# Three Strassen pairs instead of two in the third layer of a fused attention and two-layer network kernel, with two reorderings around them

## Chip, cores, metric

The kernel runs on one core of a Trainium2 chip. The metric is the device time of one execution in microseconds (us); the time before is the median of three runs.

## What is computed

Causal attention over 2 batches, 12 heads, 448 positions and head size 64, followed by two feed-forward networks with 768 inputs and 2048 hidden units on the 896 tokens, all to float32 accuracy:

```python
x = attention(q, k, v)                       # (896, 768)
h = x @ moe_w_in;  g = max(h, 0) + alpha * min(h, 0);  x = g @ moe_w_out
h = x @ moe2_w_in
g = where(h >= 1, h, where(h <= -1, 0, (h + 1) ** 2 / 4))
out = g @ moe2_w_out
```

## The kernel before

The program calls the four matrix products layers one to four: layer one is `moe_w_in`, layer two `moe_w_out`, layer three `moe2_w_in`, layer four `moe2_w_out`. Attention comes first and fills about the first 78 us; then the layers follow one another. The order of every instruction on every engine is written out by hand (`tc.manual_schedule()`), and each engine works off its own list in that order.

**Split operands.** TensorE gets every float32 operand as two parts, a rounded high part and the low part that is left, and does three products for one (high by high, high by low, low by high). A weight tile arrives as raw 8-byte values. GpSimd casts their upper bits to `top` (L209), VectorE joins them with the rest into a float32 tile (`join`, L218), ScalarE copies the high part (`high`, L253), and VectorE subtracts it for the low part (`low`, L257). The split weight goes into one of three `w_split` buffers.

**Layer three.** The 2048 hidden units are 16 f tiles of 128, the 768 inputs are 6 k tiles, and the tokens are two halves b of 448. A plain f tile is 6 x 2 x 3 = 36 matmuls of 448 columns into a pair of PSUM banks (`pair()`, of which there are two in rotation). `ORDER` visits the f tiles as 0, 8, 1, 9, ..., 7, 15; I number the positions of this order 0 to 15, so that positions 2k and 2k + 1 are pair k. During position i the vector engines do three things in the order of the list `ops` in `run_layer`: the activations of position i - 1 (`late[:2]`, the two squares on ScalarE, L339 and L340; `late[2:4]`, the two totals on VectorE, L345, each followed by the split of its result, L324 and L327, or by a store), the weights of position i + 2 (`a`: join, high, load, low), and what stands further back in `late`, the sums over a finished pair.

**Sums of a pair.** Layer four is itself done by Strassen's scheme. `sum_ops` gives for each pair `first` (L383, the matrix S1), `third` (L397) and `second` (L392), which are sums of activations with stores to memory, and a later accumulating DMA for S4. The activations live in six `act` buffers.

**A Strassen pair (`Fold`).** For the pairs in `FOLD[3]`, the two f tiles of a pair are computed by seven products P1 to P7 of 9 matmuls each. P1 runs inside the position before, after its fourth k tile; then P6, P5, P2, P7 and P3 run in one block; P4 runs in the middle of the position after. Bank B holds P1, then P1 + P6, and so on. What a partial sum is still needed for is copied out by ScalarE first: `keep("u1")` after P1, `keep("u2")` after P6, `keep("u5")` from bank D after P5 (all L590). P6 therefore can't begin before u1 is copied, P7 not before u2, P3 not before u5. The sums of weights that these products need are made by `sums12` (L218 join, L546, L547, L550 high, L553 low) and `sums34` (L561, L562, L564, L576), both in the position before. The first Strassen pair also makes the three right-hand sums T4 (L477, L479, L480). The right-hand sums T1 to T4 keep twelve of the 44 on-chip `places` until the last Strassen pair has read them. Where the position before a Strassen pair is the second tile of another pair, `late[4:]` with the deferred sums runs at the very end of its list.

Of the kernel before, what the change touches and what calls it, by code (L numbers as in the profile page):

```python
# [22 lines left out]
def attention_moe_moe_kernel(ctx: ExitStack, tc: tile.TileContext, qk, v, w1, w2, w3, w4, alpha, out):  # L23
# [35 lines left out]
    NPAIR = NF // 2  # L59
    WHOLE = 6  # L60
    ORDER = [f for k in range(NPAIR) for f in (k, NPAIR + k)]
# [3 lines left out]
    NU = len(STEPS) * len(PARTS)  # L65
    QUARTERS = "B11", "B21", "B12", "B22"
    LATE = {1: 0, 2: 0, 3: 0}
    FOLD = {1: (), 3: (2, 5)}
    HALF = KD // 2 * 128
    SIDES = {  # L70
# [259 lines left out]
    def activate(layer, ps, f, b):  # L330
# [11 lines left out]
        def total():  # L342
# [5 lines left out]
            if negate and layer == 3:  # L348
                nc.scalar.mul(g, g, -1.0)
            if f >= NPAIR and b and FOLD[layer]:  # L350
                keep("A22", f - NPAIR, g)
# [13 lines left out]
    def keep(n, k, t):  # L365
        d = sums[n, k] = spill.tile([128, S], F32, tag=f"{n}_{k}", name=f"d{n}_{k}")
        nc.sync.dma_start(out=d, in_=t)
# [6 lines left out]
    def sum_ops(layer, k):  # L374

        tiles = []
        late = layer == 1 and FOLD[1] or layer == 3 and k or k >= NPAIR - 2

        def first():
            g11, g12, g21, g22 = (parts.pop((b, f)) for b in range(NB) for f in (k, NPAIR + k))  # L380
            s1 = act_tile("s1")
            tiles.extend((g11, g21, s1))
            nc.vector.tensor_sub(s1, g21, g22)  # L383
            keep("S4", k, g12)
            lows.extend(split_g(left_tile("S1", k), s1, k + 1 == NPAIR))
            if not late:
                keep("S3", k, g21)
                keep("S2", k, s1)

        def second():  # L390
            g11, _, s1 = tiles
            nc.vector.tensor_add(g11, s1, g11)  # L392
            keep("S2", k, g11)

        def third():
            g11, g21, _ = tiles
            nc.vector.tensor_add(g21, g21, g11)  # L397
            keep("S3", k, g21)

        last = [lambda: add("S4", k, sums["S2", k])] * (k < NPAIR - 2)  # L400
        if late:
            return [first, third, second], [], last
        return [first], [lambda n=n: add(n, k, tiles[0]) for n in ("S2", "S3")], last
# [20 lines left out]
    def pair(pool=None):  # L424
        return (pool or ps_s).tile([128, 2, 512], F32, tag="s", name="ps")
# [4 lines left out]
    def products(ps, ws, src, k, kk, first, last):  # L430

        for part in range(2):
            for b in ps:
                for xp in range(2 - part):
                    nc.tensor.matmul(  # L435
                        ps[b][:, :S],
                        lhsT=ws[:, part, k * 128:(k + 1) * 128],
                        rhs=src[b, kk][:, xp],
                        start=first and part == 0 and xp == 0,
                        stop=last and part == 1,  # L440
                    )
# [184 lines left out]
    def run_layer(layer, late):  # L626

        deferred, last = [], []
        folds = {k: Fold(layer, k, k == max(FOLD[layer])) for k in FOLD[layer]}
        fold, skip = None, 0  # L630
        for i, f in enumerate(ORDER):
            if skip:
                skip = 0
                continue
            if f in folds:
                fold, skip = folds[f], 1
                wts.next()
                for name in ("P6", "P5", "P2"):
                    fold.step(name)
                wts.fill()  # L640
                a, w, w4 = later.ahead(i), fold.second(), fold.split4()
                fourth = [lambda k=k: rights.total("T4", k, nc.gpsimd) for k in range(MH) if f == min(FOLD[layer])]
                c22, c12, c21, c11 = (fold.output(n) for n in ("C22", "C12", "C21", "C11"))
                for ops in ([w4[0], *late[:2], a[0], w4[1], *late[2:4], lambda: fold.keep("u2", "B"), lambda: fold.step("P7")],
                            [a[1], *a[2:], lambda: fold.keep("u5", "D"), lambda: fold.step("P3")],
                            [w[0], c11[0], w[1], *fourth, c22[0], c11[1], *late[4:5], c11[2]]):
                    for op in ops:
                        op()
                late, pending = [*c12, *late[5:], *c22[1:], *deferred], last
                deferred, last = [], []  # L650
                continue
            if layer == 1 and f in early:
                ws, ps = early.pop(f)
                products(ps, ws, x_t, KD - 1, KD - 1, False, True)
                wts.run(wts.load())
            else:
                ws, t = wts.next(), pair()
                ps = {b: t[:, b] for b in range(NB)}
                if layer == 3 and i == 0:
                    for b in range(NB):  # L660
                        ks = [(k + MH * b) % KD for k in range(KD)]
                        for k in ks:
                            products({b: t[:, b]}, ws, x_t, k, k, k == ks[0], k == ks[-1])
                else:
                    for k in range(KD):
                        if k == MH and fold:
                            fold.step("P4")
                        if k == MH + 1:
                            if i + 1 < NF and ORDER[i + 1] in folds:
                                folds[ORDER[i + 1]].start()  # L670
                                folds[ORDER[i + 1]].step("P1")
                        products(ps, ws, x_t, k, k, k == 0, k == KD - 1)
            if wts.n_used > 1:
                wts.fill()
                if i + 1 < NF and ORDER[i + 1] in folds:
                    new = folds[ORDER[i + 1]]
                    a, b = new.sums12(), new.sums34()
                    ops = [*late[:2], a[0], *late[2:4], a[1], lambda: new.keep("u1", "B"), *a[2:], *b, *late[4:]]
                else:
                    a = later.ahead(i - bool(fold))  # L680
                    if fold:
                        ops = [late[0], a[0], late[1], a[1], late[2], *a[2:], *late[3:]]
                    else:
                        ops = [*late[:2], a[0], *late[2:4], a[1], *late[4:5], *a[2:], *late[5:]]
                for op in ops:
                    op()
                if fold:
                    wts.fill()
                    a = later.ahead(i)
                    now, deferred, last = sum_ops(layer, fold.k)  # L690
                    for op in [a[0], c21[0], a[1], c21[1], *a[2:], now[0]]:
                        op()
                    deferred = [*now[1:], *pending, *deferred]
                    fold = None
            for kind, name in SIDES[layer].get(i, ()) if FOLD[layer] else ():
                for k in range(MH):
                    getattr(rights, kind)(name, k)
            late = [op for two in zip(*(activate(layer, ps[b], f, b) for b in range(NB))) for op in two]
            now, before, deferred, last = [], deferred, last, []
            if f >= NPAIR:  # L700
                now, deferred, last = sum_ops(layer, f - NPAIR)
            late += now + before
        for b in range(NB):
            for m in range(KD):
                places.put(f"x{b}", m)
        return late + deferred + last

    class Strassen:
# [9 lines left out]
        def __init__(self, layer):  # L718
            self.layer = layer
            self.f, self.ws, self.bank, self.u = {}, {}, {}, {}  # L720
            self.names = ("S2", "S4", "S3") + ("A22",) * bool(FOLD[layer - 1])

# [362 lines left out]
    with tc.manual_schedule():  # L1085
# [132 lines left out]
        late = []  # L1218
        for layer in (1, 3):
            later = Strassen(layer + 1)  # L1220
            later.run(run_layer(layer, late))
            late = []
# [44 lines left out]
```

## Time and profile before

| | |
|---|---|
| median of three runs | 516.12 us (513.93 to 519.12) |
| profiled execution, its time | 515.88 us |
| profiled execution, its span | 514.1 us |
| TensorE busy | 507.3 us, 99% of the span |
| VectorE busy | 391.0 us, 76% |
| ScalarE busy | 315.4 us, 61% |
| GpSimd busy | 281.6 us, 55% |
| mean granted TensorE clock | 0.997 |

The time of an execution is its span and 1.8 us around it. The span is from the first to the last instruction that the profiler recorded. Matmuls are pipelined: one takes 365 ns from start to end, but the next starts after about 203 ns, so the time of a block is read from the starts of the blocks.

### The profile page before, as it was taken

Reading aid. Unit: us, or ns where it says so; the run is one execution under the profiler, and the core shown is the slowest. Engines: PE = TensorE matmul, PEld = TensorE weight load, DVE = VectorE, ACT = ScalarE, POOL = GpSimd, SP = SyncE. Lnnn points to the kernel's source line nnn. Section 1 sums busy time; section 2 is a strip of 40 time slices with the busy share of each in tenths; the row PEclk is TensorE's granted clock in tenths of the full one; section 3 lists DMA queues with packets and bytes.
Section 4 is the critical chain, followed back from the end, with each engine's and each line's share of the span. In section 5 each row is a group of like instructions: output and inputs, shape, how many; then the busy total and the mean of one; then the engine's idle time right before and its main releaser. Section 6 shows DMA issues by size and latency. Waiting matters only on the chain.

```text
span 514.1 us, 8592 instructions
## 1 busy us (share of the span) xinstructions
PE 507.3 (99%) x2893; PEld 445.8 (87%) x2893; DVE 391.0 (76%) x639; ACT 315.4 (61%) x641; POOL 281.6 (55%) x361
## 2 busy tenths in 40 slices
PE   8999999999999999999999999999999999999997
PEld 4656668999999999999999999898999999999996
DVE  5799876655565599896788689788888898967881
ACT  6899974665556558556643366676677675555531
POOL 7667745667766693325212398586355823480450
PEclk9899999999999999999999999999999999999999
DMA  6646505577778979899344745948568997892211
GB/s 194 191 136 212 158 9 185 178 215 192 164 212 209 225 212 338 279 264 345 122 108 113 211 144 167 222 137 248 177 187 252 290 364 281 244 320 92 73 55 54
DMA packets 46396, 99.97 MB, mean 194 GB/s; under 512 B 6400, under 2 KB 34688, under 8 KB 46352
## 3 DMA queue, kind: packets, MB, share of 16 engines
q1 hardware_dynamic: 35808, 75.69, 43.8%
q0 software_dynamic: 9824, 23.17, 20.4%
q10 hardware_dynamic: 720, 0.56, 0.3%
q8 instruction: 23, 0.38, 0.3%
q14 instruction: 21, 0.17, 0.1%
HBM read 75.09 MB, written 22.48 MB: 190 GB/s over the span
## 4 chain that ended last, share of the span: by engine, by line
PE 87%; DVE 4%; POOL 4%; ACT 3%; issue 2%; DVEq 0%; ACTq 0%; POOLq 0%
PE ps L788 40%; PE ps L435 31%; PE ps L1076 4%; PE ps L997 4%; PE ps L1059 3%; PE ps L522 2%; POOL T L480 2%; PE ps L990 2%; POOL top L209 1%; PE ps L109 1%; DVE g L345 1%; DVE w_split L257 1%; POOL pexp L1034 1%; DVE ps L218 0%; ACT g L339 0%
## 5 line engine op out<-in xcount | busy, mean ns | idle before, releaser
L435 PE MATMUL ps<-x,w_split 128*128 128x448 f32 x1008 | 206.3, 366 | 0.5 <-DVE g L345 0.5
L435 PEld LDWEIGHTS ps<-x,w_split 128*128 128x128 f32 x1008 | 189.1, 188 | 15.9 <-DVE g L345 0.8
L788 PE MATMUL ps<-S,w_split 128*128 128x448 f32 x576 | 117.1, 365 | 0.0
L788 PEld LDWEIGHTS ps<-S,w_split 128*128 128x128 f32 x576 | 108.2, 188 | 8.6
L788 PE MATMUL ps<-A,w_split 128*128 128x448 f32 x432 | 88.2, 365 | 0.0
L788 PEld LDWEIGHTS ps<-A,w_split 128*128 128x128 f32 x432 | 81.1, 188 | 6.4
L327 POOL TENSOR_TENSOR A<-g,A 128x448 fp32r<-128x448 f32 x37 | 49.1, 1334 | 55.6 <-ACT A L324 52.0
L754 ACT CAST w_split<-B 128x768 fp32r<-128x768 f32 x42 | 35.1, 836 | 59.8 <-PE ps L788 25.7
L345 DVE SCALAR_TENSOR_TENSOR g<-ps,g 128x448 f32<-128x448 f32 x62 | 37.9, 622 | 44.2 <-ACT g L335 35.3
L758 DVE TENSOR_TENSOR w_split<-B,w_split 128x768 fp32r<-128x768 f32 x42 | 42.2, 1004 | 19.1 <-ACT w_split L754 18.8
L209 POOL CAST top<-w_raw 128x768 f16<-128x768 bf16 x34 | 48.5, 1428 | 7.3 <-DVE ps L218 6.5
L1034 POOL TENSOR_SCALAR pexp<-pexp,stat 128x384 f32<-128x384 f32 (+3 forms) x79 | 38.9, 513 | 16.5 <-DVE stat L1026 8.3
L1017 ACT ACTIVATE pexp<-pexp,stat 128x128 f32<-128x128 f32 (+3 forms) x84 | 43.7, 524 | 5.6 <-DVE stat L1008 5.2
L195 POOL CAST top<-w_raw 128x256 f16<-128x256 bf16 (+1 forms) x27 | 22.7, 840 | 42.7 <-DMA w_raw<-w 34.8
L335 ACT ACTIVATE g<-ps 128x448 f32<-128x448 f32 x32 | 17.1, 536 | 38.3 <-PE ps L435 38.3
L1008 DVE CUSTOM_DVE_ANT_0 pexp<-ps,mask 128x128 f32<-128x128 f32 (+3 forms) x84 | 33.0, 448 | 6.0 <-POOL ident masks.py:199 3.5
L257 DVE TENSOR_TENSOR w_split<-ps,w_split 128x768 fp32r<-128x768 f32 x27 | 25.8, 955 | 13.7 <-ACT w_split L253 13.4
L218 DVE SCALAR_TENSOR_TENSOR ps<-w_raw,top 128x768 uint32<-128x768 uint32 x27 | 32.4, 1199 | 1.2
L826 POOL DMA_DIRECT2D S<-dS x48 | 26.4, 556 | 9.5 <-PE ps L788 7.4
L842 DVE TENSOR_TENSOR S<-S 128x448 fp32r<-128x448 f32 x48 | 30.3, 656 | 0.0
L324 ACT CAST A<-g 128x448 fp32r<-128x448 f32 x40 | 22.6, 567 | 10.0 <-DVE g L345 8.5
L327 POOL TENSOR_TENSOR S<-s,S 128x448 fp32r<-128x448 f32 x14 | 23.7, 1693 | 7.6 <-ACT S L324 7.6
(127 smaller groups left out, 711.3 us busy)
## 6 DMA issues: line engine op xcount, KB each, us to landing
w_raw<-w SPq DMA_DIRECT2D x29, 767.8 KB, 5.6
w_raw<-w SPq DMA_DIRECT2D x51, 255.8 KB, 5.3
w_raw<-w SPq DMA_DIRECT2D x24, 511.8 KB, 5.2
S<-dS POOLq DMA_DIRECT2D x48, 224.0 KB, 5.4
dS<-g SPq DMA_DIRECT2D x41, 224.0 KB, 4.4
qk<-qk SPq DMA_DIRECT2D x10, 448.0 KB, 3.6
dS<-dS POOLq DMA_DIRECT2D x16, 224.0 KB, 6.1
dS<-g POOLq DMA_DIRECT2D x14, 224.0 KB, 4.9
```

Of the source, the lines that this page charges most:

```text
L209: (side.copy if side is nc.scalar else side.tensor_copy)(d[:, c], src[:, c])
L218: nc.vector.scalar_tensor_tensor(out=w[:, a:b], in0=t.rearrange("p (n two) -> p n two", two=2)[:, c, 0], scalar=13, in1=top[:, c], op0=ALU ...
L257: (side or nc.vector).tensor_sub(s[:, 1, c], w()[:, c], f32(s[:, 0, c]))
L327: nc.gpsimd.tensor_sub(t[:, 1, :], g, f32(t[:, 0, :]))
L345: nc.vector.scalar_tensor_tensor(out=g, in0=ps[:, :S], scalar=floor, in1=g, op0=ALU.max, op1=last, reverse1=negate and layer == 1)
L435: nc.tensor.matmul(ps[b][:, :S], lhsT=ws[:, part, k * 128:(k + 1) * 128], rhs=src[b, kk][:, xp], start=first and part == 0 and xp == 0, st ...
L754: nc.scalar.copy(s[:, 0], w)
L758: nc.vector.tensor_sub(s[:, 1], w, f32(s[:, 0]))
L788: nc.tensor.matmul(ps[:, :S], lhsT=ws[:, part, (at + k - ks[0]) * 128:(at + k - ks[0] + 1) * 128], rhs=left[name, k][:, xp], start=first a ...
L1008: nc.vector.tensor_tensor_reduce(out=self.pexp[p][:, o:o + w], in0=b[:, :w], in1=mask3 if i == 3 else mask[:, 384 - w:], scale=-SCALE, sca ...
L1017: nc.scalar.activation(out=e, in_=e, func=AF.Exp, bias=self.st[p][:, 0, n:n + 1], scale=-1.0, accum_out=self.st[p][:, 1, n:n + 1],)
L1034: nc.gpsimd.tensor_scalar(out=e, in0=e, scalar1=self.st[p][:, 2, n:n + 1], scalar2=1.0, op0=ALU.mult, op1=ALU.mult)
```

## The change

Three edits. The Strassen pairs of layer three become pairs 2, 4 and 6 instead of 2 and 5. In the list of a Strassen pair, the copy of bank B to u2 moves ahead of the low part of S4 and of the two totals of the position before. In the list of a plain position that neither follows nor precedes a Strassen pair, the fifth entry of `late` stays ahead of the load and the low part of the weights only where the position before is a pair's second tile; elsewhere it now comes behind them.

```diff
-    FOLD = {1: (), 3: (2, 5)}
+    FOLD = {1: (), 3: (2,4,6)}
...
-                for ops in ([w4[0], *late[:2], a[0], w4[1], *late[2:4], lambda: fold.keep("u2", "B"), lambda: fold.step("P7")],
+                for ops in ([w4[0], *late[:2], a[0], lambda: fold.keep("u2", "B"), w4[1], *late[2:4], lambda: fold.step("P7")],
                             [a[1], *a[2:], lambda: fold.keep("u5", "D"), lambda: fold.step("P3")],
                             [w[0], c11[0], w[1], *fourth, c22[0], c11[1], *late[4:5], c11[2]]):
...
-                        ops = [*late[:2], a[0], *late[2:4], a[1], *late[4:5], *a[2:], *late[5:]]
+                        n = 5 if i and ORDER[i - 1] >= NPAIR else 4
+                        ops = [*late[:2], a[0], *late[2:4], a[1], *late[4:n], *a[2:], *late[n:]]
```

## Rows read from the trace of the kernel before

**Rows 1.** The page, busy time of each engine.

```profile
PE 507.3 (99%) x2893; PEld 445.8 (87%) x2893; DVE 391.0 (76%) x639; ACT 315.4 (61%) x641; POOL 281.6 (55%) x361
```

**Rows 2.** Chain that ended last, layers three and four: start us, us, what.

```profile
368.08 9.12 PE ps L522 x45
...
408.21 102.16 PE ps L788 x504
```

**Rows 3.** Waits of the weight loads, 293.8 to 410: us in total, times, longest.

```profile
PEld ps L435 <- DVE g L345: 0.8, 1, 0.8
PEld ps L522 <- DVE w_split L553: 0.5, 1, 0.5
PEld ps L522 <- ACT u L590: 0.3, 1, 0.3
```

**Rows 4.** Timeline of PE, 310 to 360: start, us, instructions, count, [idle before].

```profile
324.64 4.20 PE L522 MATMUL ps<-T,w_split 128*128 128x448 f32 x18
328.67 1.99 PE L522 MATMUL ps<-x,w_split 128*128 128x448 f32 x9
330.60 2.09 PE L522 MATMUL ps<-T,S 128*128 128x448 f32 x9
...
339.82 11.11 PE L435 MATMUL ps<-x,w_split 128*128 128x448 f32 x54
351.40 8.78 PE L435 MATMUL ps<-x,w_split 128*128 128x448 f32 x42 [0.47 <-DVE g L345]
```

**Rows 5.** Timeline of ScalarE, first Strassen pair and positions 7 and 8.

```profile
329.55 0.57 ACT L324 CAST A<-g 128x448 fp32r<-128x448 f32 x1 [0.39 <-DVE g L345]
...
348.32 0.63 ACT L339 ACTIVATE g<-ps,half 128x448 f32<-128x448 f32 x1
...
350.11 0.58 ACT L340 ACTIVATE g<-g 128x448 f32<-128x448 f32 x1
...
355.24 0.64 ACT L339 ACTIVATE g<-ps,half 128x448 f32<-128x448 f32 x1 [0.30 <-DVE g L392]
```

**Rows 6.** Timeline of VectorE, position 7, then the second Strassen pair.

```profile
347.73 0.96 DVE L218 SCALAR_TENSOR_TENSOR ps<-w_raw,top 128x768 uint32<-128x768 uint32 x1
350.11 1.24 DVE L345 SCALAR_TENSOR_TENSOR g<-ps,g 128x448 f32<-128x448 f32 x2 [1.42 <-ACT g L339]
...
361.78 1.25 DVE L546 TENSOR_TENSOR F<-F 128x384 f32<-128x384 f32 x1
363.07 0.55 DVE L547 TENSOR_TENSOR F<-F,ps 128x384 f32<-128x384 f32 x1
```

**Rows 7.** Timeline of ScalarE, the second Strassen pair, and position 13.

```profile
365.21 0.82 ACT L550 CAST w_split<-F 128x768 fp32r<-128x768 f32 x1
...
372.20 0.53 ACT L590 COPY u<-ps 128x448 f32<-128x448 f32 x1
372.63 0.80 ACT L253 CAST w_split<-ps 128x768 fp32r<-128x768 f32 x1
...
388.05 0.63 ACT L339 ACTIVATE g<-ps,half 128x448 f32<-128x448 f32 x1
```

**Rows 8.** Single lines of VectorE: duration ns min/median/max, first and last start.

```profile
L553 DVE TENSOR_TENSOR w_split<-F,w_split x2: 1703/1942/2180, 323.1 to 366.1; 128x768 fp32r<-128x768 f32 x2
...
L392 DVE TENSOR_TENSOR g<-s,g x9: 624/1461/1748, 185.3 to 416.1; 128x448 f32<-128x448 f32 x9
...
L397 DVE TENSOR_TENSOR g<-g x9: 615/715/1577, 184.3 to 415.4; 128x448 f32<-128x448 f32 x9
...
L257 DVE TENSOR_TENSOR w_split<-ps,w_split x13: 946/958/960, 291.1 to 392.4; 128x768 fp32r<-128x768 f32 x13
```

**Rows 9.** Timeline of GpSimd at 361 us.

```profile
361.32 1.35 POOL L209 CAST top<-w_raw 128x768 f16<-128x768 bf16 x1
```

**Rows 10.** Timeline of all engines, first units of layer four.

```profile
414.55 0.96 DVE L758 TENSOR_TENSOR w_split<-B,w_split 128x768 fp32r<-128x768 f32 x1
...
416.31 0.73 POOL L195 CAST top<-w_raw 128x256 f16<-128x256 bf16 x1 [4.32 <-DMA w_raw<-w]
```

## Prediction

> **What bounds the kernel now.** I read the page's busy times first: TensorE is busy for 507.3 us, and no other engine comes near it [rows 1]. The chain that ended last then gives the price of a matmul. A block of 504 in layer four takes 102.16 us, and the block of 45 in a Strassen pair takes 9.12 us [rows 2]. Both come to 202.7 ns from start to start, so no matmul is cheap and none is dear: time goes with their number. The third view is what the weight loads waited for in layer three: only three waits, on a total of VectorE, on the low part of the summed weights, and on the copy u2 [rows 3]. The timeline of PE says what they cost, as the start of the next block less the count of matmuls at 0.2027 us. P6 and P5 (18) start at 324.64 and P2 at 328.67, 4.03 us where 3.65 is needed: 0.38 lost. P2 to P7 takes 1.93 us instead of 1.82: 0.11 lost. The 54 matmuls from 339.82 should end at 350.77, and position 8 starts at 351.40: 0.63 lost [rows 4]. So the kernel is a TensorE bound one with 1.1 us of stalls in this layer, and the two edits of order can at most give back what is stalled. Everything else has to come from fewer matmuls, or be lost to new stalls.
>
> **The third Strassen pair: what it removes.** A plain pair is 72 matmuls, a Strassen pair 7 x 9 = 63. There is one more of them: 9 x 0.2027 = 1.82 us less. The stall of 0.63 us at position 8 has no place any more: position 8 was a plain tile that waited for its PSUM pair, and in its stead P6 runs, which needs bank B; the pair is taken by P5, 1.8 us later, when position 6 has long been read. I take it as gone, and cost what is late next below.
>
> **What it adds.** Beside the matmuls a Strassen pair gives VectorE seven more instructions on 384 columns (L546, L547, L561, L562 and three of L576) and three totals on 448, ScalarE three copies of a bank and three of weights. At 0.55 us [rows 6] and about 0.6 us these are some 6 us of VectorE in 12.8 us. They cost nothing as long as each ends before its product. For pair 5 before, they did: no wait of rows 3 falls there. What differs now is where the pairs stand. Pair 4 begins two positions after pair 2, and the vector engines are still behind from that one: at position 7, which starts at 339.82 + 18 x 0.2027 = 343.47, the first square of position 6 starts only at 348.32, nearly 5 us late, and the totals end at 351.35 [rows 5, 6]. In the kernel before this lag cost the 0.63 us. Now position 7 also has to make the sums for P6.
>
> The chain for P6 of pair 4, in time of the profile before. TensorE: position 7 with P1 in it is 45 matmuls, so P6 is due at 343.36 + 9.12 = 352.5 (0.11 us earlier by the stall at P7, which edit two removes, see there). Vector engines: ScalarE idled 0.39 us before L324 in the first pair [rows 5]; edit two puts u2 there, so I let all that follows start 0.4 us earlier. The join runs from 347.3 to 348.3, L546 takes 0.55 to 1.25, L547 0.55 [rows 6], so the sums end at 349.4 to 350.1. The squares end at 350.3, the two totals at 350.7 to 351.5, and the two ScalarE instructions behind them (0.57 each, as L324) at 351.3 to 352.1. Then the high part, 0.82 [rows 7], ends at 352.1 to 352.9 and u1, 0.53, at 352.6 to 353.4. P6 writes u1's bank, so it can't start earlier: 0.1 to 0.9 us. The low part L553 starts behind the high part. It took 1.70 and 2.18 us in the two cases of the trace; the nearest instruction of that size, L257, took 0.96 in all 13 [rows 8]. So it ends between 353.1 and 355.1, and P6 needs it at its third matmul, due at 352.9. **Stall at P6: 0.2 to 2.2 us; I take 1.1**, nearer to the row of 1.70 than to that of 0.96.
>
> That choice hangs on GpSimd. The L546 of the second pair took 1.25 us beside a GpSimd cast that ran from 361.32 to 362.67, and the L547 right after it, of the same size but with one operand in PSUM, took 0.55 [rows 6, 9]. The Trainium skill (GPSIMD Engine Reference, section 8, Key points) says that GpSimd shares its SBUF interfaces with VectorE and contends with instructions that have two SBUF inputs. By that rule this change is worse placed than its count of instructions says, since L546, L553, the three of L576, `third` and `second`, on which the products of pair 4 wait, all read two SBUF inputs. The trace agrees with L546 and L547. By the rule alone the low part would be put at its upper row (2.18) and the sum would be 0.5 us higher; the rows between decide, because the GpSimd cast of that position need not fall on it.
>
> **P7 and P3 of pair 4, and edit two.** Behind the low part (354.0, the middle) VectorE has L561, L562 and S3's low part, 1.7 us, to 355.7. New is what stands at the end of position 7's list: `third` and `second` of pair 2, 0.62 to 1.58 and 0.62 to 1.75 us [rows 8]. They end at 356.9 to 359.0. ScalarE's second square needs a free `act` buffer; before, the square at the same place started only when L392 had ended [rows 5]. I take the same here: the square and its second half (1.24) end at 358.2 to 360.3, u2 (0.53) at 358.7 to 360.8. P7 is due 27 matmuls after P6: 352.5 + 1.1 + 5.5 = 359.1. So P7 loses 0 to 1.7. Here edit two matters: without it u2 would also stand behind a join (0.95), S4's low part (0.55), a total (0.62) and L324 (0.57), of which 1 to 2 us would show. P3 is due 1.82 us after P7 and needs u5, which stands behind the first total, L324, the high part (0.80) and its own copy: 361.0 to 363.1, against 360.9 to 362.6: 0.1 to 0.5 more. **I take 0.4 for both (0 to 2.2)**, since the upper end needs `third` and `second` both at their longest. P4 and the weights of position 10 come about 1 us before they are needed, or more.
>
> **Edit two in the pairs before**: the 0.11 us at P7 of pair 2 goes. Queued behind u2 on ScalarE are L324 and the high part, which start 0.5 us later or fill an idle time; the GpSimd low part behind L324 has no one waiting soon.
>
> **Pair 6.** The vector engines carry a smaller lag into it, because pair 4 has no T4 totals (three L477, three L479, three L480, which only the first Strassen pair makes). By the trace of pair 5, whose next position starts its squares at 388.05 [rows 7], 1.7 us after TensorE (368.08 + 9.12 + 45 x 0.2027 = 386.3 [rows 2]) instead of nearly 5, and some 1.6 us that pair 4 inherits, P6 is met to within 0.2. A count of places shows that the last free one goes to u1 of pair 6, and that S4's high part takes a place of T2, so ScalarE waits there for P6's second k tile, about 0.4 us. **0.2 us (0 to 1.5).**
>
> **Edit three.** In layer one the entry that moves is a DMA issue on GpSimd, and what it changes places with runs on SP and VectorE: no engine's order changes. In layer three only position 15 is touched: `third` of pair 6 comes behind the low part of layer four's second unit, not ahead of it. No DMA changes its order on SP or GpSimd by it. Those weights are needed 3.65 us (18 matmuls) after the end of the layer. **Nothing, from -0.2 to 0.5.** What covers it is the lead of the weights in layer four: the low part at 414.55 is for its fourth unit, which starts at 408.21 + 54 x 0.2027 = 419.2 [rows 2, 10].
>
> **Sum**, on the profiled execution: 515.88 - 1.82 - 0.63 - 0.11 + 1.1 + 0.4 + 0.2 = **515.0 us**. The median of the runs is 0.24 us above that execution, which is far less than their spread (513.93 to 519.12), so I leave it out.
>
> **Rivals.**
> - *The stalls stay away.* L553 is never seen free of GpSimd, and could take 0.96; then pair 4 loses 0.2 to 0.4 and nothing else: 515.88 - 2.56 + 0.3 = 513.6. For it: at pair 5 all was met with over 1 us to spare. Against it: the lag of 5 us at position 7 and both durations of L553. Chance 0.25.
> - *Slower: the deferred sums ahead of pair 4's middle.* `third` and `second` sit between S3's and S4's low parts, with a square behind them on ScalarE and P7 behind that. If they end later than about 357.3, u2 comes after P7 is due, and each us goes straight to TensorE; u5 and the position after follow. With all at the upper ends: 2.2 + 2.2 + 1.5 - 2.56 = 3.3 over, 519.2; from half of that it is slower than before, 516 to 518. Against it: two long instructions in a row need GpSimd busy throughout. Chance 0.14.
> - *It doesn't do what it says: TensorE's gain is handed back in layer four.* The first casts there wait up to 4.32 us for a DMA of weights [rows 10]. If memory sets the pace, TensorE only arrives earlier and waits: 516 us. Against it: the weights then lie over 4 us ahead (419.2 against 415.5). Chance 0.06.
>
> My forecast, part of the saving given back, has 0.55: 514.3 to 516. The range of 8 in 10 reaches to the first rival with half of the spread of the runs and into the second: 512.9 to 517.9. A measurement of this kernel tells about 1% (5.2 us) from no change. More than 5.2 us faster has no case among these and more than 5.2 slower only the worst end of the second, so both are left to the spread: 0.03 and 0.04, and 0.93 for no change.
>
> **What would show it.** In the profile after: 45-matmul blocks three times, at pairs 2, 4 and 6, and 549 + 504 matmuls from the start of layer three; no wait at a plain position 8; a wait of PE for L553 or for a u copy (L590) near 352.5, the largest of the layer; smaller ones at P7 or P3; a second square there that ends its idle time on L392; nothing at pair 2's P7; layer four with no new wait. Wrong would be the prediction if pair 4 shows no stall (then 513.6), or if the stalls sum to over 2.6 us.

## Result and the profile after

The changed kernel takes 520.61 us (median of 9 runs, 518.45 to 521.25) against 515.79 us for the kernel before (9 runs): **ratio 1.0082, interval 1.0055 to 1.011**. The forecast was 515.0, range 512.9 to 517.9, no change within 1%. The size is inside 1%, but the sign is wrong and the time is outside the range. Ratios, here and below, are taken over all runs of both kernels; they are not the quotient of the two medians, which is 1.0093 here.

The profiled execution took 520.84 us. What answers to rows 3, the waits of the weight loads (layer four's line is one further down than before, L789):

```profile
PEld ps L789 <- DVE w_split L759: 3.0, 2, 2.3
PEld ps L522 <- DVE w_split L553: 2.9, 3, 1.8
...
PEld ps L522 <- ACT u L590: 0.9, 1, 0.9
...
PEld ps L789 <- ACT w_split L755: 0.5, 1, 0.5
```

The wait on a total has gone, the one on L553 has grown from 0.5 to 2.9 us, and the first line is new: TensorE waits in layer four. For the sizes I read the change by stages, from the timeline of TensorE: where layer three starts, where layer four starts, and where the last block of 72 matmuls starts. The kernel before:

```profile
293.63 6.65 PE L435 MATMUL ps<-x,w_split 128*128 128x448 f32 x32
...
408.05 29.35 PE L788 MATMUL ps<-A,w_split 128*128 128x448 f32 x144
437.23 58.53 PE L788 MATMUL ps<-S,w_split 128*128 128x448 f32 x288
495.60 14.75 PE L788 MATMUL ps<-A,w_split 128*128 128x448 f32 x72
```

The changed kernel:

```profile
291.78 26.91 PE L435 MATMUL ps<-x,w_split 128*128 128x448 f32 x132
...
348.07 2.60 PE L435 MATMUL ps<-x,w_split 128*128 128x448 f32 x12
351.24 0.67 PE L522 MATMUL ps<-T,w_split 128*128 128x448 f32 x2 [0.57 <-ACT u L590]
353.36 3.51 PE L522 MATMUL ps<-T,w_split 128*128 128x448 f32 x16 [1.45 <-DVE w_split L553]
356.70 1.99 PE L522 MATMUL ps<-x,w_split 128*128 128x448 f32 x9
358.53 1.99 PE L522 MATMUL ps<-T,S 128*128 128x448 f32 x9
...
380.42 0.57 PE L522 MATMUL ps<-T,w_split 128*128 128x448 f32 x2
381.23 3.51 PE L522 MATMUL ps<-T,w_split 128*128 128x448 f32 x16 [0.25 <-DVE w_split L553]
...
406.47 4.21 PE L789 MATMUL ps<-A,w_split 128*128 128x448 f32 x20
412.63 8.71 PE L789 MATMUL ps<-A,w_split 128*128 128x448 f32 x34 [1.95 <-DVE w_split L759]
421.51 0.68 PE L789 MATMUL ps<-A,w_split 128*128 128x448 f32 x2 [0.17 <-ACT w_split L755]
422.51 18.42 PE L789 MATMUL ps<-A,w_split 128*128 128x448 f32 x88 [0.32 <-DVE w_split L759]
440.76 59.68 PE L789 MATMUL ps<-S,w_split 128*128 128x448 f32 x288
500.28 15.04 PE L789 MATMUL ps<-A,w_split 128*128 128x448 f32 x72
```

| profiled execution | before | after |
|---|---|---|
| layer three starts | 293.63 | 291.78 |
| layer three, to the start of layer four | 114.42 | 114.69 |
| layer four, to the start of its last block | 87.55 | 93.81 |
| span | 514.1 | 519.1 |

The 1.85 us ahead of layer three are the spread of executions, for up to there no engine runs its instructions in another order; in the execution of before the granted clock was at its half level for a stretch during attention (0.50 from 14 to 16 us). **Layer three is no shorter, though it has nine matmuls less, and layer four, where the diff does no more than move one sum ahead of it, is 6.3 us longer.**

In layer three the positions can be read off as in [rows 4]. P6 of pair 4 is due at 348.07 + 12 x 0.2027 = 350.50, starts at 351.24, stops after two matmuls for L553 and goes on at 353.36 instead of 351.65: 0.74 and 1.71, 2.45 us lost. P7 follows P2 after 1.83 us, no stall. P6 of pair 6 loses 0.4. So 1.82 + 0.63 + 0.11 saved and 2.85 lost make +0.3.

In layer four a unit of weights is 18 matmuls, and the third of each unit is the first that needs the low part. For the second unit that is due at 406.47 + 20 x 0.2027 = 410.5 and starts at 412.6 (2.1 lost). The 34 matmuls from there take 8.7 us instead of 6.9. The windows show why:

```profile
411.00:418.00 7.00, 5.37 (x19) 4.84 (x20) 6.00 (x7) 4.06 (x7) 5.72 (x9) 0.76 0.82 200
418.00:425.00 7.00, 6.51 (x31) 5.39 (x30) 5.47 (x8) 3.61 (x6) 1.08 (x2) 1.00 1.05 410
```

The columns are the stretch, its length, the busy time (and count) of PE, PEld, DVE, ACT and POOL, the granted clock, the DMA share and GB/s. After the idle stretch the clock is at 0.76 of full speed in the mean of 411 to 418, a mix of its two levels, 1.2 and 2.4 GHz, and back at 1.00 in the next window: 1.8 us. About 0.8 us are waited near 421.5. The rest is stranger: from 422.51 to 500.28 the 376 matmuls come every 206.8 ns, at granted clock 1.00, where before they came every 202.7 [rows 2]: 1.5 us. The sum, 6.2, is the lengthening.

What made the second unit's low part late is in the timelines of the changed kernel around the seam of the two layers (start, length, engine, line, instruction, idle time before and what ended it):

```profile
400.21 1.26 DVE L218 SCALAR_TENSOR_TENSOR B_None<-w_raw,top 128x768 uint32<-128x768 uint32 x1 [2.08 <-POOL top L209]
401.39 0.61 DVE L345 SCALAR_TENSOR_TENSOR g<-ps,g 128x448 f32<-128x448 f32 x1
...
402.39 0.38 SPq L367 DMA_DIRECT2D dA<-g  x1
...
408.00 0.63 ACT L339 ACTIVATE g<-ps,half 128x448 f32<-128x448 f32 x1 [2.85 <-DMA dA<-g]
...
408.67 1.24 DVE L345 SCALAR_TENSOR_TENSOR g<-ps,g 128x448 f32<-128x448 f32 x2 [5.26 <-ACT g L339]
409.82 0.95 DVE L218 SCALAR_TENSOR_TENSOR B<-w_raw,top 128x768 uint32<-128x768 uint32 x1
410.69 1.89 DVE L759 TENSOR_TENSOR w_split<-B_None,w_split 128x768 fp32r<-128x768 f32 x1
...
419.50 0.63 DVE L383 TENSOR_TENSOR s<-g 128x448 f32<-128x448 f32 x1 [2.46 <-DMA dS<-g]
```

Read upwards from PE's wait: the low part of the second unit (L759) ends at 412.6. It stands behind the totals of position 14, these behind a square (L339), and that square waits 2.85 us for one of the six `act` buffers, which is free only when the store of A22 of pair 6 has landed, 5.6 us after its issue at 402.39. The same again at 419.50: S1 of the last pair waits for the store behind pair 6's `third`. Pair 6 is a Strassen pair now, so its last activation (C21), its A22 store and its sums come at positions 14 and 15, when layer four's weights are already made and loaded, and not a position earlier as for a plain pair. The same store, square and low part in the kernel before:

```profile
396.91 0.33 SPq L367 DMA_DIRECT2D dA<-g  x1
...
402.35 0.64 ACT L339 ACTIVATE g<-ps,half 128x448 f32<-128x448 f32 x1 [0.15 <-DMA dA<-g]
...
405.62 1.91 DVE L758 TENSOR_TENSOR w_split<-B_None,w_split 128x768 fp32r<-128x768 f32 x1
```

There the store was issued 11.1 us ahead of layer four, now 4.1 us. A square waited for it there too, but for 0.15 us, and the low part was ready at 407.5, 4.6 us before TensorE needed it.

### The profile page after: what moved, and what is told of

It is laid out like the page before. It is cut to its first block, busy times and chain, and to the rows that moved or that the text cites. A ratio compares the mean times of both kernels' runs of the same rounds, so it can differ in the third digit from the quotient of the medians.

```text
span 519.1 us, 8599 instructions
## 1 busy us (share of the span) xinstructions
PE 507.7 (98%) x2884; PEld 444.1 (86%) x2884; DVE 395.0 (76%) x649; ACT 317.2 (61%) x647; POOL 281.2 (54%) x361
## 4 chain that ended last, share of the span: by engine, by line
PE 75%; POOL 7%; issue 6%; DVE 5%; DMA 3%; ACT 2%; ACTq 0%; SPq 0%; POOLq 0%; DVEq 0%
PE ps L789 38%; PE ps L435 24%; PE ps L1077 4%; PE ps L998 3%; PE ps L1060 3%; POOL T L480 2%; POOL top L209 2%; PE ps L522 2%; PE ps L991 2%; POOL A L327 1%; DMA dS<-g 1%; DMA dA<-g 1%; DVE w_split L553 1%; POOL S L327 1%; DMA qk<-qk 1%
## 5 line engine op out<-in xcount | busy, mean ns | idle before, releaser
L435 PE MATMUL ps<-x,w_split 128*128 128x448 f32 x936 | 191.9, 366 | 0.0
L435 PEld LDWEIGHTS ps<-x,w_split 128*128 128x128 f32 x936 | 175.8, 188 | 13.9
L789 PE MATMUL ps<-S,w_split 128*128 128x448 f32 x576 | 118.2, 367 | 0.0
L789 PEld LDWEIGHTS ps<-S,w_split 128*128 128x128 f32 x576 | 108.2, 188 | 9.7
L789 PE MATMUL ps<-A,w_split 128*128 128x448 f32 x432 | 91.2, 372 | 2.4 <-DVE w_split L759 2.3
L789 PEld LDWEIGHTS ps<-A,w_split 128*128 128x128 f32 x432 | 82.1, 191 | 10.9 <-DVE w_split L759 3.0
L327 POOL TENSOR_TENSOR A<-g,A 128x448 fp32r<-128x448 f32 x37 | 47.4, 1288 | 60.3 <-ACT A L324 57.4
L759 DVE TENSOR_TENSOR w_split<-B,w_split 128x768 fp32r<-128x768 f32 x42 | 41.8, 996 | 15.9 <-ACT w_split L755 15.5
L195 POOL CAST top<-w_raw 128x256 f16<-128x256 bf16 (+1 forms) x27 | 24.3, 899 | 44.4 <-DMA w_raw<-w 26.1
```

The costliest lines, as they stand in the source:

```text
L327: nc.gpsimd.tensor_sub(t[:, 1, :], g, f32(t[:, 0, :]))
L435: nc.tensor.matmul(ps[b][:, :S], lhsT=ws[:, part, k * 128:(k + 1) * 128], rhs=src[b, kk][:, xp], start=first and part == 0 and xp == 0, st ...
L759: nc.vector.tensor_sub(s[:, 1], w, f32(s[:, 0]))
L789: nc.tensor.matmul(ps[:, :S], lhsT=ws[:, part, (at + k - ks[0]) * 128:(at + k - ks[0] + 1) * 128], rhs=left[name, k][:, xp], start=first a ...
```

## Experiments

The theory after this reading: two separate losses, one at P6 of pair 4 (two positions behind pair 2), one at the seam (the last Strassen pair at position 12). Against it stood the mere amount of vector work of three Strassen pairs, and the memory: TensorE outrunning the weights of layer four. The kernel before was run again beside each group of runs: its median was 516.02 us beside the first four below, 516.26 beside the next four and 514.34 beside the last two.

**Pairs 2 and 6**, with both edits of order:

```diff
-    FOLD = {1: (), 3: (2,4,6)}
+    FOLD = {1: (), 3: (2, 6)}
```

> Strassen pairs 2 and 6, with the two edits of order, so as many matmuls as in the kernel before. Theory (place of the last pair): pair 6 at position 12 puts its sums and its A22 store into positions 14 and 15, where a store from an act buffer takes over 5 us; a square waits for the buffer and the weights of layer four's second unit come late. Then layer four loses 2 to 6.5 us here too, and the time is 1 to 6 us above before, although pair 6 has no pair close ahead of it; layer three loses nothing at pair 6. Rival one (amount: three Strassen pairs are too much work for VectorE and ScalarE): two pairs are not too much, so as before within 1 us. Rival two (memory: TensorE outruns the weights of layer four when layer three is shorter): layer three is not shorter, so as before within 1 us.

519.45 us, ratio 1.0082 (1.005 to 1.0114): the whole loss, with as many matmuls as before and with no pair close ahead of pair 6. Layer three takes 113.99 us. In layer four the same two stops stand in PE's timeline, and its length to the last block is 94.55 us, 7.0 more than before, a little over the 2 to 6.5 that were expected:

```profile
407.29 4.21 PE L789 MATMUL ps<-A,w_split 128*128 128x448 f32 x20
413.02 7.16 PE L789 MATMUL ps<-A,w_split 128*128 128x448 f32 x34 [1.52 <-DVE w_split L759]
421.53 0.67 PE L789 MATMUL ps<-A,w_split 128*128 128x448 f32 x2 [1.35 <-ACT w_split L755]
```

Amount and memory both fall: two pairs and a layer three that is only 0.4 us shorter give the full loss. It is the place of the last pair.

**Pairs 2 and 4**, with both edits of order:

```diff
-    FOLD = {1: (), 3: (2,4,6)}
+    FOLD = {1: (), 3: (2, 4)}
```

> Strassen pairs 2 and 4, with the two edits of order, as many matmuls as before. Theory: pair 4 two positions behind pair 2 loses about 2.5 us at P6 as in the changed kernel, less the 0.7 us of stalls at position 8 and P7 that go: 1 to 2.5 us slower than before; layer four runs without a stall, 102.2 us. Rival one (amount): as before within 1 us. Rival two (memory): as before.

517.22 us, ratio 1.0036 (1.0006 to 1.0066). Layer three takes 116.03 us, 1.6 more than before; P6 of pair 4 waits as in the changed kernel; layer four runs 87.55 us to its last block, as before. The loss at P6 of pair 4 stands alone here, with the size that was expected, and the seam loses nothing without a Strassen pair at position 12.

**Two more buffers.** The two activations of position 14 go to free on-chip places instead of the six `act` buffers; all work stays.

```diff
-        g = parts[b, f] = act_tile("g")
+        spare = layer == 3 and f == NPAIR - 1
+        g = parts[b, f] = f32(places.take(f"g{b}", f))[:, 0, :] if spare else act_tile("g")
```

(and `places.put` behind the stores in `second` and `third`).

> The changed kernel with the two activations of position 14 in free on-chip places instead of two of the six act buffers, so that the squares need not wait for a store. Theory: the wait of 2.9 us of a square at 408 goes, also that of the next pair's first sum at 419, layer four loses under 1.5 us instead of 6.6, and the time falls by 4 to 6.5 us, to 514 to 517. Rival one (amount): VectorE and ScalarE are late anyway, a gain under 1.5 us. Rival two (memory): under 1.5 us.

516.17 us, 4.4 less than the changed kernel; ratio to before 1.0023 (1.0001 to 1.0045). Layer four has no stop at all:

```profile
406.60 29.35 PE L794 MATMUL ps<-A,w_split 128*128 128x448 f32 x144
435.78 58.53 PE L794 MATMUL ps<-S,w_split 128*128 128x448 f32 x288
494.14 14.76 PE L794 MATMUL ps<-A,w_split 128*128 128x448 f32 x72
```

87.54 us to the last block, the length before. The low part of the second unit is ready at 409.8, 0.9 us before it is needed. No vector work was taken away and no DMA changed its place in a queue, so the buffers that waited for stores were the cause of the loss at the seam. (The line numbers of this kernel are up to 5 higher.)

**The cast later.** `wts.fill`, GpSimd's cast of the next weights, moves behind P7 in every Strassen pair.

```diff
-                wts.fill()
                 a, w, w4 = later.ahead(i), fold.second(), fold.split4()
...
-                for ops in ([w4[0], *late[:2], a[0], lambda: fold.keep("u2", "B"), w4[1], *late[2:4], lambda: fold.step("P7")],
+                for ops in ([w4[0], *late[:2], a[0], lambda: fold.keep("u2", "B"), w4[1], *late[2:4], lambda: fold.step("P7"), wts.fill],
```

> The changed kernel with GpSimd's cast of the next weights inside a Strassen pair issued behind P7 instead of ahead of it. Theory: the low part L553 of pair 4 then runs free of GpSimd's cast, takes 1.0 to 1.6 us instead of 2.5, and P6 of pair 4 loses 1.0 to 1.6 us less; layer four as in the changed kernel; total 1 to 2 us below the changed kernel, if no later join waits for the cast. Rival: L553 is long for a reason of its own (three SBUF operands), and stays at 1.7 to 2.5.

516.54 us, ratio to before 1.0006 (0.9982 to 1.0029). First L553 in the changed kernel at pair 4 and the cast beside it, then L553 in this run:

```profile
350.79 2.51 DVE L553 TENSOR_TENSOR w_split<-F,w_split 128x768 fp32r<-128x768 f32 x1 [1.37 <-ACT w_split L550]
...
351.23 1.30 POOL L209 CAST top<-w_raw 128x768 f16<-128x768 bf16 x1
```

```profile
L553 DVE TENSOR_TENSOR w_split<-F,w_split x3: 958/959/1184, 323.1 to 378.6; 128x768 fp32r<-128x768 f32 x3
```

From 2.51 us to 0.96 by moving another engine's instruction. P6 of pair 4 now loses 0.8 us instead of 2.45, nothing is lost at pair 6 and in the first pair, and layer three takes 112.06. That is 2.6 us less in the profile, where the expectation said 1 to 1.6 for P6 alone; the median fell by 4.1. The rest is not all accounted for: layer four still stops for 1.8 us at its second unit, but comes back to 203 ns a matmul sooner (58.53 us for its 288).

**Both cures together.**

> The changed kernel with both cures: position 14's activations in free places, and GpSimd's cast behind P7. Theory (two losses, each at its place, that add up): layer three as in the run with the later cast, P6 of pair 4 losing under 1 us, layer four without a stall, 102.2 us; the saving of 1.8 us of matmuls is then mostly kept: 513.5 to 515.2, that is 0.2 to 0.5% faster than before. Rival (amount of vector work): what is cured at one place comes back at another, and the time stays at 516.

513.03 us, ratio 0.9943 (0.9913 to 0.9972), 0.5 us under the expected times: the two losses add up, and their cures nearly do (7.6 us together, 4.4 and 4.1 alone). The rival falls. The profiled execution took 517.34 us, 4.3 more than the median, and shows the slower spacing of 206.7 ns from pair 2 on to the end, with only 0.8 us of waits for the low part and 0.4 for u1 in layer three and none in layer four:

```profile
407.50 29.92 PE L793 MATMUL ps<-A,w_split 128*128 128x448 f32 x144
437.26 59.68 PE L793 MATMUL ps<-S,w_split 128*128 128x448 f32 x288
```

**Without edit three** (`n = 5` always):

> The changed kernel without edit three: at position 15 the sum L397 runs ahead of the low part of layer four's second unit again. Theory: that low part comes 0.6 to 1.1 us later still, the stall at the second unit grows by as much, 0.5 to 1.5 us slower than the changed kernel. Rival (my prediction: the lead of the weights covers it): no difference from the changed kernel.

520.64 us, the time of the changed kernel. The wait at the second unit grew as the theory said, but the later waits went, so the expected loss did not come:

```profile
406.12 4.31 PE L789 MATMUL ps<-A,w_split 128*128 128x448 f32 x20
413.70 27.40 PE L789 MATMUL ps<-A,w_split 128*128 128x448 f32 x124 [3.27 <-DVE w_split L759]
```

Edit three moves a wait at the seam and is worth nothing here.

**Without edit two** (u2 again behind the totals):

> The changed kernel without edit two: u2 stands behind the totals again. Theory: P7 of pair 4, which met u2 with 0.5 us to spare, loses 0.5 to 1.5 us, and the first pair gets its 0.1 us back; total 0.3 to 1.5 us slower than the changed kernel, if the rest isn't late by the same amount anyway. Rival: u2 was not late, since P6's own delay gives it time: no difference.

524.53 us (4 runs), ratio 1.015 (1.0103 to 1.0198), 3.9 more than the changed kernel and more than the 0.3 to 1.5 that were expected. The waits of the weight loads:

```profile
PEld ps L522 <- ACT u L590: 3.3, 4, 1.2
PEld ps L522 <- DVE w_split L553: 2.9, 3, 1.8
```

u copies are waited for four times instead of once, at P7 of pairs 4 and 6 among them (361.56 and 390.19, each 0.5 us idle). Layer three takes 116.68 us, 2.0 more than in the changed kernel. This profiled execution also reached layer three 1.9 us later, so of the 3.9 I count 2.0 as shown for edit two.

**Only the edits of order**, pairs 2 and 5:

> Only the two edits of order, with Strassen pairs 2 and 5 as before. Theory: the edits alone do next to nothing, 0.1 to 0.4 us faster (the stall at P7 of pair 2), nothing at layer four, since edit three finds no sums to move there: ratio 0.998 to 1.001. Rival: the edits themselves cost the time: 2 us or more slower.

515.44 us, ratio 0.9989 (0.9963 to 1.0016), layer three 114.46. The edits alone do nothing that can be measured.

**High part ahead.** On top of both cures, L550 goes ahead of the two totals in the position before a Strassen pair:

```diff
-                    ops = [*late[:2], a[0], *late[2:4], a[1], lambda: new.keep("u1", "B"), *a[2:], *b, *late[4:]]
+                    ops = [*late[:2], a[0], a[1], *late[2:4], lambda: new.keep("u1", "B"), *a[2:], *b, *late[4:]]
```

> Both cures, and in the position before a Strassen pair the high part L550 stands ahead of the two totals and of the two ScalarE instructions that follow them, which waits for nothing but the sums L546 and L547. Theory (what is left of the loss at P6 of pair 4 is ScalarE's order: u1 stands behind the high part, and that behind two totals): u1 ends 0.5 to 0.6 us earlier, the low part 0.5 to 1.4 us, P6 of pair 4 loses under 0.4 us instead of 0.8; the time falls by 0.2 to 0.7 us below the run with both cures, 512.3 to 514. Rival: the totals come late by it, position 8's places and the later copy u2 with them, and nothing is gained: 513 to 514.5.

**512.34 us, ratio 0.992 (0.9888 to 0.9953): faster than both kernels**, by 0.8% than the one before by the ratio and by 0.4% between the medians; the slowest of its seven runs (512.85) is under the fastest of the 18 of the kernel before (513.86). Against both cures the medians differ by 0.7 us, but those are two sets of runs, in which the kernel before differs by 1.9; the times don't show this gain, only the trace does. PE's timeline at pair 4 and at the seam:

```profile
349.66 2.60 PE L440 MATMUL ps<-x,w_split 128*128 128x448 f32 x12
352.10 3.81 PE L527 MATMUL ps<-T,w_split 128*128 128x448 f32 x18
355.74 1.99 PE L527 MATMUL ps<-x,w_split 128*128 128x448 f32 x9
...
405.00 29.35 PE L793 MATMUL ps<-A,w_split 128*128 128x448 f32 x144
```

Layer three starts at 293.73 and takes 111.27 us, which is 549 x 0.2027 = 111.3: not one stall is left, and the weight loads wait for nothing from there to the end.

**The store on another queue.** In the changed kernel the one A22 store of pair 6 is issued from ScalarE's DMA queue.

> The changed kernel with the one store of A22 of pair 6 issued from ScalarE's DMA queue instead of SP's, where four loads of weights were issued just ahead of it. Theory one (the store is slow since it stands behind those loads in one queue): it lands in 2 to 4 us instead of 5.6, the square of position 14 waits under 1.5 us instead of 2.9, the stall at layer four's second unit goes from 2.1 to under 1 us; 1 to 4 us below the changed kernel. Theory two (all DMA engines are full at that time, whatever the queue): it lands after 5 us or more here too, and the time is as that of the changed kernel.

519.16 us, ratio 1.007 (1.0041 to 1.0098). From the chain of waits, the store, and from ScalarE's timeline, the square behind it:

```profile
404.22 5.37 DMA dA<-g
```

```profile
409.61 0.64 ACT L339 ACTIVATE g<-ps,half 128x448 f32<-128x448 f32 x1 [2.28 <-DMA dA<-g]
```

It lands after 5.4 us on its own queue too, so it is not slow because it stands behind loads in SP's queue. The second theory holds as far as it goes; that the DMA engines are full is read from their share (0.96 from 403 to 407 in this run, but 0.81 in the changed kernel), not tried. The median is 1.4 us below the changed kernel's, but so is that of the kernel before beside it, and the ratios' intervals overlap: a difference in time is not shown.

## Why the prediction was wrong

**What held.** The price of nine matmuls, 1.82 us: the run with the high part ahead has 549 at 202.7 ns each. The stall of 0.63 at position 8 went, that of 0.11 at P7 of pair 2 went (328.62 follows 326.79 by 1.83). The lag of pair 4, its place (P6, first u1, then L553's low part) and its reason (GpSimd's cast against two SBUF inputs) were as described. Here the rule of the Trainium skill (GPSIMD Engine Reference, section 8, Key points) was the better guide: it spoke for the upper row, and the trace agrees, 2.51 us beside the cast and 0.96 without it.

**Mis-sized: the stall at P6 of pair 4**, 1.1 taken (0.2 to 2.2), 2.45 measured. L553 took longer beside the cast than either time that the trace before had shown [rows 8], and the two totals began late because L546 was stretched too (1.40, where I had allowed for 1.25 at most, though the trace before has one of 1.39). Between 0.96 and 2.18 I chose by nearness, where the order of the program settled it: `wts.fill` stands in front of the Strassen pair's list, so the cast follows at once behind the GpSimd work of position 7 and falls on L553 each time (2.16 to 2.52 us in the three pairs). One of the two rows that I took for contention said nothing: L547 began at 363.07, when the cast had ended (362.67). In the changed kernel L547 does run beside a cast (347.31 to 348.71) and takes 0.56, so the reading stands, on another row. With the 0.4 of pair 6 the new stalls of layer three come to 2.85, over the 2.6 that I had named as a sign of being wrong.

**Right or nearly: P7 and P3** (0.4 taken, none measured) and pair 6 (0.2 taken, 0.4 measured, again a wait for L553). The slower rival was built on `third` and `second` ahead of P7. They took 0.62 us each, their square waited 0.26 for L392 as foreseen, and u2 was ready 0.6 us before P7. That rival named the right sign by a mechanism that did not happen.

**The step that failed** is the sentence under edit three, "What covers it is the lead of the weights in layer four", and with it the sum, which has no term for layer four. Edit three itself does cost nothing (520.64 us without it, 520.61 with it), but the third pair takes that lead away, and layer four got 6.3 us longer. The layer three that was measured would alone have given 515.88 - 2.56 + 2.85 = 516.2 us, inside the range, and the run with two more buffers takes 516.17. I looked at what edit three itself moves, and took the lead of layer four's weights from the kernel before (3.7 us at the fourth unit by 419.2 and 415.5, not the "over 4" of the third rival; 4.6 at the second), without following what a Strassen pair at position 12 puts into positions 14 and 15: C12, C22 and C21 with their activations, the A22 store and the three sums. I had seen that a square may wait for an `act` buffer [rows 5] and priced it at pair 4 only, where it waited for VectorE. At the seam it waits for a store, which takes 5.6 us there (the eight of its kind in the changed kernel took 1.9 to 7.4); the 0.15 us that a square waited for the same store in the kernel before was the sign that I didn't follow. The third rival named this place with the wrong mechanism (weights that come late from memory); the run with two more buffers left the loads of weights as they were and took the loss away.

**Not priced at all** were the two things that a stop of TensorE cost beyond its own length: 1.8 us at half clock, 1.5 us by the slower spacing. Of the 6.2 us at the seam these are more than half.

**Open** is what moves the spacing between 202.7 and 206.8 ns, and with it how much of each difference between medians is a wait and how much the spacing behind it.

## What to carry to other kernels

Moving a special stage later in a pipeline moves its leftovers (stores, deferred sums, buffers they hold) into the next stage: follow every buffer of the moved stage to its release, and price the release by the slowest transfer of the stage in which it now falls. Where two engines contend, don't take a middle price: the order of each queue says whether the two instructions meet, and moving the one that nobody waits for can be a cure; here it cost nothing that was seen. Lost time on the bounding engine can cost more than its length.

## What the runs showed of the hardware

A matmul of this form has two spacings at the same granted clock of 1.00: 58.53 us for 288 in the kernel with two more buffers, 59.68 us in the changed kernel, that is 202.7 and 206.7 ns from start to start. In the runs the change came at a stop of TensorE (near 422 in the changed kernel, at 353 in the run with two more buffers, where it went back near 381) and could last to the end; not every stop brought it (pairs 2 and 4 had the stop and kept 202.7). What decides it was not tried.

A stop of 1.95 us was followed by a stretch at half clock in the changed kernel (0.76 from 411 to 418, 0.57 from 413 to 417). The Trainium skill (TensorE: Matmul & The Clock Gate, Part 1) says that the clock falls back when the engine has been idle; the trace agrees that it did so after this stop. The run with the store on another queue stopped for 1.4 us at the same place and kept 1.00.

One VectorE instruction of 128x768 took 0.96 or 2.51 us, without and with a GpSimd cast of 1.3 us beside it: it lost 1.55 us, more than the cast itself lasted.
